# Global value rows of batches 2 and 3: from the DMA of each tile instead of a VectorE copy

## The chip, the core and the metric

The kernel runs on one core of a Trainium2 chip. The metric is device time in microseconds (us): 718.45 us, the median of three runs (717.41 to 722.96).

## What is computed

Attention over 4 batches, 8 heads, 512 local and 32 global tokens, head size 64, followed by two mixture-of-experts layers with 8 experts each. The change lies in attention. A local query attends to the 32 global keys and to the local keys at most 32 positions away:

```python
s_ll = scale * np.matmul(q_l, k_l.transpose(0, 1, 3, 2))
mask = np.abs(pos[:, None] - pos[None, :]) <= window          # window = 32
s_ll = np.where(mask, s_ll, -1000000000.0)
s_lg = scale * np.matmul(q_l, k_g.transpose(0, 1, 3, 2))
a_l = sm(np.concatenate([s_lg, s_ll], axis=-1))
out_l = np.matmul(a_l, np.concatenate([v_g, v_l], axis=2))
```

Global queries attend to everything. The 2176 token rows of 512 values then go through `_moe_ref` and `_moe2_ref`: each row is sent to the expert with the largest logit, `out[mask] = gate_w * (max(x @ w1[e], 0) @ w2[e])`.

## The kernel before

**Tiles and steps.** A local tile is 128 queries of one batch, all 8 heads; batch b has tiles 4b to 4b+3 (n = 4b + qb). Each tile is two work items, one for the even and one for the odd heads (`hg` 0 and 1), and each batch has two items of global queries (`Global`) after its first local tile (in batch 0 after its second). One Python loop over t writes all engines' instructions in order; `tc.manual_schedule()` keeps that order on every engine. In step t the item t computes its scores (matmuls to `s_`), item t-2 has its probabilities transposed (`turn`, to `pt`, copied to `pT` by ScalarE), item t's scores get their row maxima on VectorE (`soften`: `amx` and `anm` for a local tile, `mg` and `gnm` for global queries) and their exponentials on ScalarE (`pe`, `pg`), item t-3 is multiplied with the values (`values`, to `po` or `og`), item t-4's row is turned for the router (`ptx`), and router pieces follow (`pp`, `sp`, `pl`, `lg`, `at`). So TensorE, VectorE and ScalarE pass work round within each step.

**The value window.** For a tile, `vw` holds for each of 4 groups of 32 queries (`cg`) 128 value rows: two end blocks of 32 rows, 32 global rows and so on, ordered so that the even groups have end block and global rows in partitions 0 to 63 and the odd groups in 64 to 127. Three buffers `vws` are used in turn, tile n has `vws[n % 3]`. `load_windows` issues two SyncE DMAs (even groups, odd groups), which bring 32 end-block rows for two groups each, and four GpSimd copies of 64 rows from the batch's value tile. `global_values` brings the 32 global rows, by two VectorE copies from `vg`, where all batches' global values lie. Tiles 0 to 2 get them by DMA, with 64 rows for each group. Tiles 4 to 6, 8 to 10 and 12 to 14 get them by these copies. The fourth tile of a batch (3, 7, 11, 15) finds them in its buffer, which the first tile of the batch used.

**When.** After the second half of tile n-3's `values`, `load_windows` for tile n is written, and the two copies of `global_values` follow, one at the end of this step and one at the end of the next (`take(1, filling)`). Tile 12 is an exception: in step 28 its load is put behind the four loads of the first expert's `w1a` on the SyncE queue (`load1`, 512 KB each), which wait for the choice of the first expert (`first`). The second half of those weights (`w2a`) is loaded in steps 31 and 32.

Of the kernel before, what the change touches and what calls it, by code (L numbers as in the profile page):

```python
# [20 lines left out]
P = 128  # L21
# [31 lines left out]
def start_block(g):  # L53
    return (3 * g) // 2 if g % 2 == 0 else (3 * g + 1) // 2
# [51 lines left out]
def sparse_attention_two_moe(ctx, tc, qt, kt, vx, vn, qg, emb, tau, w1a, w2a, wgo, w1b, w2b, cs1, cs2, out):  # L106
# [65 lines left out]
    def take(n, *its):  # L172

        for _ in range(n):
            for it in its:
                next(it, None)
# [18 lines left out]
    def embed_turn(psp):  # L195
        pe_ = psp.tile([P, 4, 8], F32, name="pe_", tag="small")
        for k in range(4):
            T.transpose(pe_[:, k, :], em[:, k * P:(k + 1) * P], ident[:E, :E])
        V.tensor_copy(enT[:, :, :8], pe_)

    def zero_rows():

        G.memset(order[1].oh, 0.0)
        G.memset(order[1].rank, 0)
        G.memset(at[:, SMAIN:SMAX, :], 0.0)
        for i in range(2):
            G.dma_start(out=xs[i][ZROW:ZROW + 1, :], in_=zt[0:1, :])
            G.dma_start(out=gs[i][ZROW:ZROW + 1, :], in_=zrow)
        for i in range(SMAIN, SMAX):
            G.dma_start(out=xs[1][row0(i, 1):row0(i, 1) + P, :], in_=zt)  # L210
            G.dma_start(out=gs[1][row0(i, 1):row0(i, 1) + P, :], in_=zt[:, :2])
# [429 lines left out]
    def rows_of(a, n):  # L641
        return [a[:, k * n:(k + 1) * n] for k in range(4)]
# [10 lines left out]
    def keep_warm(n, psp):  # L653

        if n:
            warm = psp.tile([P, 512], F32, name="idle", tag="small")
            for i in range(n):
                T.matmul(warm, lhsT=onesb, rhs=ones, start=True, stop=True)
# [849 lines left out]
    def load_batch(b):  # L1508
        kq = big()
        kT = kq[:, :4 * EXT].rearrange("p (j n) -> p j n", j=4)  # L1510
        qT = kq[:, 4 * EXT:].rearrange("p (j n) -> p j n", j=4)
        if b == 0:

            S.dma_start(out=qT[:, :, :2 * P], in_=qt[b, :, :, :2 * P].rearrange("j p n -> p j n"))
            for k0, k1 in ((0, 288), (288, EXT)):
                SP.dma_start(out=kT[:, :, k0:k1], in_=kt[b, :, :, k0:k1].rearrange("j p n -> p j n"))
                yield
            SP.dma_start(out=qT[:, :, 2 * P:], in_=qt[b, :, :, 2 * P:].rearrange("j p n -> p j n"))
        else:
            G.dma_start(out=kT, in_=kt[b].rearrange("j p n -> p j n"))  # L1520
            G.dma_start(out=qT, in_=qt[b].rearrange("j p n -> p j n"))
        held[b] = (kT, qT)
        yield

    def load_values(b):

        if b == B - 1:  # L1530
            room = gp.tile([P, 4, DM], F32, name="room")
            halves_ = [room[:, :2], room[:, 2:]]
        elif b == 2:
            halves_ = [st2[i] for i in range(2)]
        else:
            halves_ = [st1[2 * b + i].rearrange("p (j d) -> p j d", j=2) for i in range(2)]
        held[b, "v"] = [a[:, j, :] for a in halves_ for j in range(2)]
        for i, a in enumerate(halves_):
            (G if b else SP).dma_start(out=a, in_=vn[b, :, 2 * i:2 * i + 2])
            yield  # L1540

    def load_windows(b, qb):

        n = 4 * b + qb
        vw = vws[n % 3]
        for par in range(2):
            r0 = start_block(4 * qb + par) * 32  # L1550
            p0, p1 = ((P - 64, P) if par else (0, 64)) if n < 3 else ((96, P) if par else (0, 32))
            SP.dma_start(out=vw[p0:p1, par:4:2, :], in_=strided(vx[b], r0 + p0, p1 - p0, 96, 2))
        v = held[b, "v"][qb]
        for cg, to, of in ((0, 64, 0), (1, 0, 0), (2, 64, 64), (3, 0, 64)):
            G.tensor_copy(vw[to:to + 64, cg, :], v[of:of + 64])
        held[b, qb] = vw
# [7 lines left out]
    def strided(rows_, r0, n, step, m):  # L1564

        a = rows_[r0:r0 + n, :]
        return bass.AP(tensor=a.tensor, offset=a.offset, ap=[a.ap[0], [step * DM, m], a.ap[1]])
# [163 lines left out]
    for b in range(B):  # L1731
        loc = [("L", b, qb, hg) for qb in range(4) for hg in range(2)]
        n = 2 if b else 4
# [28 lines left out]
    for t in range(len(items) + 3):  # L1762
        if t - 7 in routes:
            routes[t - 7][0].gather(routes[t - 7][1])
        if t < len(items):
            it = items[t]
            if it[0] == "G":
                live[t] = live[t - 1].second if it[2] else Global(it[1])
            else:
                b, qb, hg = it[1:]  # L1770
                if hg == 0:
                    sums = sm.tile([P, H], F32, name="sums", bufs=3)
                if hg == 0 and qb == 0 and 0 < b < B - 1:
                    take(1, load_batch(b + 1))
                    take(2, load_values(b + 1))
                live[t] = Local(b, qb, hg, live[t - 1] if hg else None, sums)
            live[t].scores()
        if t < 6:
            keep_warm(3, ps_m)
        if 2 <= t < 6:  # L1780
            take(4, emb_norm)
        if t == 4:
            for i in range(1, 3):
                SP.dma_start(out=vg[i * SG:(i + 1) * SG, 1:], in_=vx[1:, 32:64, :].rearrange("b p d -> p b d"))
        if t == 22:
            SP.dma_start(out=wg[:, :, :16], in_=wgo.rearrange("p (k e) -> p k e", k=4))
            zero_rows()
        if t == 6:
            embed_turn(ps_m)
            V.tensor_copy(trib, d[:, C_TRI:C_TRI + P])  # L1790
            V.tensor_copy(order[0].val, d[:, C_VAL:C_VAL + len(TILES)])
            V.tensor_copy(order[0].gt[:, :, 1], d[:, C_TOK:C_TOK + len(TILES)])
        if t == 28:
            chosen = first.choose(acc1, ps_m, "small")
            take(1, chosen)
        if t == 32:
            take(1, found)
            first.rows = row0(8)
        if t - 2 in live:
            live[t - 2].turn()  # L1800
        if t < len(items):
            live[t].soften()
        if 28 <= t < 31:
            take(1, chosen)
        if t == 28:
            first.load()
        if t - 3 in live:
            done = live.pop(t - 3)
            r = done.values()
            if r is not None:  # L1810
                routes[t - 3 + 3 * isinstance(done, Global)] = r
            if t == len(items) + 2:
                groups[3].norm2()
            if not isinstance(done, Global) and done.hg == 1:
                n = done.b * 4 + done.qb + 3
                if 4 <= n < 16 and n % 4 < 3:
                    filling = global_values(n // 4, n % 4)
                if t == 28:

                    awaited = n // 4, n % 4  # L1820
                elif n < 16:
                    load_windows(n // 4, n % 4)
        if t == 28:
            load1(w1a, first.ex)
            load_windows(*awaited)
        elif t in (31, 32):
            load2(w2a, first.ex, range(2 * t - 62, 2 * t - 60))
        if t - 4 in routes:
            routes[t - 4][0].turn(routes[t - 4][1])
            routes[t - 4][0].store_rows(routes[t - 4][1])  # L1830
        if t - 5 in routes:
            routes[t - 5][0].multiply(routes[t - 5][1])
        take(1, filling)
        if t == 31:
            found = first.find(range(8), ps_m, "small", 8)
            take(1, found)
        if t == 31:
            w1h = rows_of(big().bitcast(F32R), F)
        if 31 <= t < 35:
            G.tensor_copy(w1h[t - 31], st1[t - 31])  # L1840
        if t == 35:
            sl[0].gather(0)
            sl[0].gather_gate(0)
        if t == 36:
            gx.close()
            wp = ctx.enter_context(tc.tile_pool(name="wp", bufs=1, side="right"))
            w2h = [wp.tile([P, 2, DM], F32R, name=f"w2h{k}") for k in range(4)]
            w2l = []
            sl[0].xT = wp.tile([P, 4, P], F32, name="xT0")
        if t == 40:  # L1850
            w1l = rows_of(big().bitcast(F32R), F)
        if t == 40:
            sl[0].turn_first()
            halves = sl[0].mm1_parts()
        if t == 42:
            take(2, halves)
        if t == 39:
            V.tensor_copy(groups[4].xr[0], xg)
        order[0].mark(1)
        stages(t, t == len(items) + 1)  # L1860
# [119 lines left out]
```

## Time and profile before

| | us |
|---|---|
| median of 3 runs (lowest, highest) | 718.45 (717.41, 722.96) |
| the profiled execution | 717.52 |
| its span, first to last instruction | 715.7 |
| TensorE busy | 642.1 (90%) |
| VectorE busy | 424.0 (59%) |
| ScalarE busy | 366.1 (51%) |
| GpSimd busy | 212.6 (30%) |
| mean granted TensorE clock | 0.969 of full speed |

PE is TensorE's matmuls and PEld its weight loads, DVE is VectorE, ACT ScalarE, POOL GpSimd, and SPq the queue on which SyncE issues DMAs. A bracket at the end of a timeline row gives the idle time of the engine just before it and what ended it; "issue" stands where the engine waited for nothing that the profile shows. Attention ends at about 155 us: the last `po` matmul starts at 153.5 us. Everything after it is the two expert layers. Batches 2 and 3 of attention stand between about 70 and 155 us.

### The profile page before, as it was taken

How to read it: one execution, taken by the hardware profiler on the slowest of the kernel's cores; microseconds unless marked ns; L12 is line 12 of the kernel's file. 1: busy time of each engine (PE TensorE's matmuls, PEld its weight loads, DVE VectorE, ACT ScalarE, POOL GpSimd, SP SyncE). 2: the span in 40 equal slices, each digit the busy share in tenths (PEclk: the TensorE clock that was granted, in tenths of full speed). 3: DMA queues.
4: the chain of work that ended last, by engine and by line, in shares of the span. 5: the costliest groups of instructions: out<-in, count | busy, mean ns of one | idle time of the engine just before them, and what ended most of it. 6: DMA issues, size and time to landing. Idle time of an engine off the chain costs nothing. (4 is left out here: it accounts for less than half of the span.)

```text
span 715.7 us, 20133 instructions
## 1 busy us (share of the span) xinstructions
PE 642.1 (90%) x6255; PEld 513.0 (72%) x6263; DVE 424.0 (59%) x1210; ACT 366.1 (51%) x885; POOL 212.6 (30%) x292
## 2 busy tenths in 40 slices
PE   7787775887899989989898988989999999999994
PEld 3465554654878878868786777668887988788883
DVE  3567869668515666368667776772574555474350
ACT  2676767662424724256358654332674544474540
POOL 3452644403712122122220230032233334324131
PEclk9989989899999999999999999999999999999998
DMA  9975848423247613655586444524757444735400
GB/s 268 270 272 174 287 102 231 146 61 63 62 150 210 209 60 72 211 181 168 146 268 158 142 149 134 163 75 142 290 188 246 161 164 167 264 122 211 148 24 28
DMA packets 55290, 117.88 MB, mean 165 GB/s; under 512 B 13815, under 2 KB 15607, under 8 KB 55104
## 3 DMA queue, kind: packets, MB, share of 16 engines
q1 hardware_dynamic: 44688, 87.21, 38.8%
q0 software_dynamic: 9344, 27.91, 12.5%
q8 instruction: 86, 1.41, 0.8%
q14 instruction: 100, 0.82, 0.6%
q10 hardware_dynamic: 1072, 0.53, 0.3%
HBM read 100.11 MB, written 16.30 MB: 163 GB/s over the span
## 5 line engine op out<-in xcount | busy, mean ns | idle before, releaser
L646 DVE TENSOR_TENSOR kq<-st,kq 128x1024 fp32r<-128x1024 f32 x64 | 75.2, 1219 | 64.3 <-ACT kq L769 53.8
L1097 PE MATMUL py<-w2h,hh 128*128 128x512 f32 x304 | 88.7, 413 | 0.0
L1097 PE MATMUL py<-w2l,hh 128*128 128x512 f32 x304 | 83.2, 394 | 0.4 <-DVE w2l L646 0.4
L646 DVE TENSOR_TENSOR w2l<-st,w2h 128x1024 fp32r<-128x1024 f32 x64 | 74.1, 1218 | 12.3 <-ACT w2h L769 8.0
L684 POOL DMA_INDIRECT xrow<-xs,idx x40 | 51.7, 1294 | 59.6 <-DVE ge L582 42.9
L957 PE MATMUL ph<-kq,xh 128*128 128x512 f32 x256 | 64.4, 405 | 4.1 <-DVEq L848 1.0
L1097 PEld LDWEIGHTS py<-w2l,hh 128*128 128x128 f32 x304 | 56.9, 188 | 14.6 <-DVE w2l L646 1.3
L1169 POOL DMA_INDIRECT out<-yr,ti x21 | 23.6, 1123 | 145.5 <-issue 34.9
L1097 PE MATMUL py<-w2h,hl 128*128 128x512 f32 x232 | 63.5, 395 | 0.0
L684 POOL DMA_INDIRECT gt<-gs,idx x40 | 53.1, 1328 | 19.1 <-issue 8.9
L957 PEld LDWEIGHTS ph<-kq,xh 128*128 128x128 f32 x256 | 48.1, 192 | 14.5 <-issue 1.1
L769 ACT CAST kq<-st 128x1024 fp32r<-128x1024 f32 x56 | 55.9, 1047 | 4.5 <-ACTq L744 2.6
L769 ACT CAST w2h<-st 128x1024 fp32r<-128x1024 f32 x56 | 54.5, 1049 | 5.6 <-ACTq L831 2.0
L1097 PEld LDWEIGHTS py<-w2h,hh 128*128 128x128 f32 x304 | 51.7, 189 | 7.3 <-ACT w2h L769 0.2
L902 PE MATMUL ph<-xh,kq 128*128 128x256 f32 x384 | 50.7, 293 | 5.9 <-ACTq L761 3.1
L700 POOL TENSOR_SCALAR va<-gt 128x1 f32<-128x1 f32 x21 | 5.2, 247 | 167.8 <-DVE oh L1203 167.4
L1111 ACT ACTIVATE yr<-py,gt 128x512 f32<-128x512 f32 x38 | 26.1, 688 | 54.1 <-PE py L1097 30.2
L902 PEld LDWEIGHTS ph<-xh,kq 128*128 128x128 f32 x384 | 48.5, 200 | 7.1 <-ACTq L761 3.7
L902 PE MATMUL pht<-xh,kq 128*128 128x256 f32 x384 | 48.2, 281 | 4.4 <-DVEq L761 2.3
L1097 PEld LDWEIGHTS py<-w2h,hl 128*128 128x128 f32 x232 | 43.5, 188 | 10.4
L902 PEld LDWEIGHTS pht<-xh,kq 128*128 128x128 f32 x384 | 45.4, 188 | 6.9 <-ACTq L761 2.9
L989 ACT COPY hs<-ph 128x512 f32<-128x512 f32 x32 | 17.2, 590 | 56.5 <-PE ph L999 29.6
(544 smaller groups left out, 1278.1 us busy)
## 6 DMA issues: line engine op xcount, KB each, us to landing
st<-in_w1a SPq DMA_DIRECT2D x32, 512.0 KB
st<-in_w2a SPq DMA_DIRECT2D x32, 512.0 KB
st<-in_w1b SPq DMA_DIRECT2D x32, 512.0 KB
st<-in_w2b SPq DMA_DIRECT2D x32, 512.0 KB
xs<-yr SPq DMA_DIRECT2D x21, 256.0 KB
kq<-in_kt POOLq DMA_DIRECT2D x3, 1728.0 KB, 9.3
xs<-xrow SPq DMA_DIRECT2D x17, 256.0 KB
vw<-in_vx SPq DMA_DIRECT2D x26, 128.0 KB
```

The costliest lines, as they stand in the source:

```text
L646: eng.tensor_sub(lo[k], st[k], hi[k].bitcast(F32))
L684: G.indirect_dma_start(out=to, out_offset=None, in_=rows_[self.l][:n, :], in_offset=bass.IndirectOffsetOnAxis(ap=idx, axis=0), bounds_chec ...
L700: G.tensor_scalar(out=self.va[s], in0=tok, scalar1=FAR, scalar2=None, op0=ALU.is_lt)
L769: S.copy(hi[k], st[k])
L902: T.matmul(po, lhsT=w[k][:, f * P:(f + 1) * P], rhs=x[:, k, at], start=first and k == 0 and f % 2 == 0, stop=last and k == 3, skip_group_c ...
L957: T.matmul(ph[n], lhsT=x[:, k, s % XR], rhs=ws[k][n][part], start=first and k == 0, stop=last and k == 3, skip_group_check=True)
L989: S.copy(self.h[s][n], ph[n])
L1097: T.matmul(py, lhsT=hT[k][x], rhs=w[k // 2][:, k % 2], start=first and k == 0, stop=k == 7, skip_group_check=True)
L1111: S.activation(yr, py, AF.Copy, scale=gate)
L1169: G.indirect_dma_start(out=out, out_offset=bass.IndirectOffsetOnAxis(ap=self.ti.pop(s), axis=0), in_=yr, in_offset=None, bounds_check=NTOK ...
```

## The change

For tiles 8, 9, 10, 12, 13 and 14 `load_windows` lets each of its two DMAs bring 64 partitions instead of 32 (end block and global rows, which lie side by side in `vx`), and `global_values` is called for tiles 4, 5 and 6 alone.

```diff
-            p0, p1 = ((P - 64, P) if par else (0, 64)) if n < 3 else ((96, P) if par else (0, 32))
+            whole = n < 3 or 8 <= n and qb < 3
+            p0, p1 = ((P - 64, P) if par else (0, 64)) if whole else ((96, P) if par else (0, 32))
             SP.dma_start(out=vw[p0:p1, par:4:2, :], in_=strided(vx[b], r0 + p0, p1 - p0, 96, 2))
...
-                if 4 <= n < 16 and n % 4 < 3:
+                if 4 <= n < 7:
                     filling = global_values(n // 4, n % 4)
```

On VectorE, in step 30 and 31 (tile 13's copies; `xrow` is the finished row of tile 10, `fb`, `so` and `fto` belong to the search for the first expert's rows, `lg` to the router, `mg` to the global scores of batch 3), before:

```order
L1633 TENSOR_TENSOR xrow<-po,rs 128x512
L234 COPY sp_2354<-pp_2349 128x128
L1561 COPY vw_180<-vg 32x2x512
L276 TENSOR_SCALAR at<-d,pf,val_102 128x128
L1561 COPY vw_180<-vg 32x2x512
L457 TENSOR_TENSOR fb<-oh_99,fone 128x64
L459 TENSOR_REDUCE so<-fb 128x8
```

and with the change (its lines from 1552 on have numbers higher by one):

```order
L1634 TENSOR_TENSOR xrow<-po,rs 128x512
L234 COPY sp_2346<-pp_2341 128x128
L276 TENSOR_SCALAR at<-d,pf,val_102 128x128
L457 TENSOR_TENSOR fb<-oh_99,fone 128x64
L459 TENSOR_REDUCE so<-fb 128x8
```

The two copies are gone and the order of the rest is the same. This is so at all twelve places.

On the SyncE queue, in steps 28 to 30 (`st` takes the expert's weights, `vw_179` is tile 12's window and `vw_180` tile 13's), before:

```order
L219 DMA st_3_93<-in_w1a 128x1024
L1552 DMA vw_179<-in_vx 32x2x512 x2
L400 DMA gs_68<-gt_103 128x4x2
L405 DMA xs_66<-xrow 128x512
L1552 DMA vw_180<-in_vx 32x2x512 x2
```

and with the change:

```order
L219 DMA st_3_93<-in_w1a 128x1024
L1553 DMA vw_179<-in_vx 64x2x512 x2
L400 DMA gs_68<-gt_103 128x4x2
L405 DMA xs_66<-xrow 128x512
L1553 DMA vw_180<-in_vx 64x2x512 x2
```

Each of these DMAs has 64 partitions in place of 32; the order is unchanged. TensorE, ScalarE and GpSimd keep their order too.

## Rows read from the trace of the kernel before

**Rows 1.** The page, part 1: busy time, share of the span, instructions

```profile
PE 642.1 (90%) x6255; PEld 513.0 (72%) x6263; DVE 424.0 (59%) x1210; ACT 366.1 (51%) x885; POOL 212.6 (30%) x292
```

**Rows 2.** Instructions of line 1561: count, ns min/median/max, first and last start, shape

```profile
L1561 DVE COPY vw<-vg x18: 683/684/1008, 33.2 to 124.3; 32x1024 f32<-32x1024 f32 x18
```

**Rows 3.** Timeline of VectorE, 74 to 88 us: start, us, line, operation, idle before

```profile
74.07 0.80 DVE L1561 COPY vw<-vg 32x1024 f32<-32x1024 f32 x1
...
75.15 0.68 DVE L1601 TENSOR_REDUCE amx<-s__1514 128x4 f32<-128x512 f32 x1
...
81.16 0.68 DVE L1670 TENSOR_REDUCE mg<-s__1647 128x1 f32<-128x512 f32 x1
...
87.93 0.28 DVE L1691 COPY pgT<-t2g 32x128 f32<-32x128 f32 x1 [1.84 <-PE t2g L1687]
```

**Rows 4.** Timeline of TensorE and ScalarE, 74 to 86 us

```profile
74.81 0.66 PE L1615 MATMUL pt<-ident,pe 128*128 128x128 f32 x4 [0.35 <-ACT pT L1617]
...
83.06 0.69 ACT L1678 ACTIVATE pg<-s__1647,gnm 128x512 f32<-128x512 f32 x1 [0.84 <-DVE gnm L1673]
...
85.10 0.66 PE L309 MATMUL ptx<-ident,xrow 128*128 128x128 f32 x4 [1.59 <-ACT pg L1679]
```

**Rows 5.** Timeline of TensorE, 89 to 99 us

```profile
89.96 0.30 PE L232 MATMUL pp<-xT,enT 128*32 128x128 f32 x1 [1.18 <-issue]
...
94.62 0.31 PE L1701 MATMUL og<-st,pgT 128*32 128x64 f32 x5
...
98.34 1.07 PE L1701 MATMUL og<-st,pgT 128*32 128x64 f32 x27 [3.42 <-issue]
```

**Rows 6.** Stretches: length; PE, PEld, DVE, ACT, POOL busy; PEclk; DMA; GB/s

```profile
88.00:90.00 2.00, 0.82 (x40) 0.54 (x32) 1.85 (x6) 0.76 (x3) 0.54 (x1) 1.00 1.06 338
...
98.00:100.00 2.00, 1.66 (x43) 1.23 (x42) 0.16 (x1) 1.44 (x9) 0.00 (x0) 0.50 0.01 3
```

**Rows 7.** Timeline of VectorE, 112 to 129 us

```profile
112.08 0.68 DVE L1601 TENSOR_REDUCE amx<-s__2261 128x4 f32<-128x512 f32 x1
...
116.78 0.68 DVE L1561 COPY vw<-vg 32x1024 f32<-32x1024 f32 x1
...
117.84 0.69 DVE L1561 COPY vw<-vg 32x1024 f32<-32x1024 f32 x1
...
123.61 1.71 DVE L1561 COPY vw<-vg 32x1024 f32<-32x1024 f32 x2
...
128.57 0.28 DVE L1691 COPY pgT<-t2g 32x128 f32<-32x128 f32 x1 [3.05 <-PE t2g L1687]
```

**Rows 8.** Timeline of TensorE, 111 to 125 us

```profile
111.37 0.65 PE L1615 MATMUL pt<-ident,pe 128*128 128x128 f32 x4
...
119.60 0.34 PE L465 MATMUL pi<-fto,at 128*128 128x1 f16 x8 [0.90 <-DVE lg L324]
...
121.75 0.30 PE L1625 MATMUL po<-vw,pT 128*32 128x64 f32 x2
...
122.57 0.65 PE L1625 MATMUL po<-vw,pT 128*32 128x64 f32 x30 [0.52 <-DMA vw<-in_vx]
...
124.37 0.66 PE L309 MATMUL ptx<-ident,xrow 128*128 128x128 f32 x4 [1.16 <-ACT pg L1679]
```

**Rows 9.** Timeline of the SyncE queue, 109 to 112 us

```profile
109.20 2.14 SPq L219 DMA_DIRECT2D st<-in_w1a  x4
...
111.45 0.97 SPq L1552 DMA_DIRECT2D vw<-in_vx  x2
```

**Rows 10.** Stretches of 2 us, the same columns, 112 to 122 us

```profile
112.00:114.00 2.00, 2.00 (x77) 1.47 (x76) 1.97 (x5) 0.99 (x4) 1.22 (x2) 1.00 1.05 391
...
118.00:120.00 2.00, 1.10 (x42) 0.80 (x27) 1.49 (x7) 0.51 (x2) 0.00 (x0) 1.00 1.58 210
...
120.00:122.00 2.00, 2.00 (x50) 1.36 (x48) 1.93 (x7) 0.58 (x1) 0.34 (x1) 1.00 0.58 77
```

**Rows 11.** The page, part 3: queue, kind, packets, MB, share of 16 engines

```profile
q8 instruction: 86, 1.41, 0.8%
```

## The prediction

> **What bounds the kernel now.** The page's busy times come first: TensorE is busy for 642.1 us [rows 1], nearly the whole run, and most of that is the expert layers, which the change does not touch. A microsecond that attention ends earlier or later should therefore move the end by a microsecond. So I looked at the list of line 1561's instructions and then at the timelines of batches 2 and 3, engine by engine, for what TensorE waits for there. The reader is to see that it is fed in turns: VectorE's row maxima free ScalarE's exponentials, and these free the next turn on TensorE. At two places it waits for something else, a pause with no visible cause and the window load of tile 12; both are taken up below.
>
> **What goes.** Line 1561 has 18 copies with a median of 684 ns [rows 2]. Twelve go, two for each of tiles 8, 9, 10, 12, 13 and 14: 12 × 0.684 = 8.2 us of VectorE, 1.1% of the run. That is the ceiling of what the copies alone can give, if each stood on the path to the end. Their places say how many do.
>
> *Tiles 8 and 9.* Tile 8's second copy runs at 74.07 for 0.80 us, and the maxima of the next scores start at 75.15 [rows 3]. They could not have started before these scores were done. TensorE starts its next work at 74.81 after 0.35 us of idle [rows 4], so the scores ended by 74.46, and removing the pair gains 75.15 - 74.46 = 0.69 us, not 1.4. Tile 9's two copies stand ahead of the global maxima at 81.16 [rows 3]. These release ScalarE's `pg` at 83.06, which had then been idle for 0.84 us [rows 4]; before that ScalarE was at work on what the first 0.69 us also advance. So tile 9's pair (2 × 0.684 = 1.37 us) gives at most these 0.84. TensorE's `ptx` at 85.10 had waited 1.59 us for `pg` [rows 4], and it takes the whole 0.69 + 0.84 = **1.53 us**.
>
> *The pause behind it.* TensorE then stops in the middle of a group: 5 matmuls of `og`, 3.42 us of nothing, then the other 27 [rows 5]. A smaller stop of 1.18 us precedes it [rows 5]. The profile names no one who ended either. If these stops stay where they are in TensorE's own order, they move with it and the 1.53 us survive. If they last until the transfers ahead of them are through, the gain is swallowed, and the added bytes of tiles 9 and 10 make it worse: 4 DMAs × 131,072 B (32 partitions × 2 groups × 2048 B each) at the 338 GB/s of that time [rows 6] are 524,288 / 338,000 = 1.55 us. The two ends are thus -1.53 and +1.55. I take -1.53, because the 1.18 us stop ended inside the stretch 88 to 90 us with the DMA share at 1.06 [rows 5, 6], with transfers still running. Against it stands that by 98 to 100 us, where the long stop ends, the share is 0.01 [rows 5, 6].
>
> *Tiles 12 and 13.* VectorE's maxima at 112.08 [rows 7] wait behind tile 12's copies; their scores ended by about 111.4, where TensorE goes on with `pt` at 111.37 [rows 8], so 0.7 us is to be had. Tile 13's copies, at 116.78 and 117.84 [rows 7], hold up `lg`, for which TensorE waits 0.90 us before 119.60 [rows 8]. Together TensorE would come to tile 12's values 0.7 + 0.9 = 1.6 us earlier, at 121.75 - 1.6 = 120.15.
>
> *What waits there.* Tile 12's load stands on the SyncE queue at 111.45, behind four loads of 512 KB from 109.20 on [rows 9], and it is already late. TensorE does two matmuls of `po` at 121.75 and then stops for 0.52 us, until the window is in, at 122.57 [rows 8]. The start of these loads is set by the choice of the first expert, ahead of which no copy of batch 3 stands, so it doesn't move against the steps around it. The load now carries 262,144 B more. No row has the price, so I bound it by the GB/s of the stretches around: 0.67 us at 391, 3.40 us at 77, and 1.16 us at the mean of 391, 210 and 77 [rows 10], which is 226. I take 1.16, because the load is in flight through all three. A gain is excluded for the load itself, as no byte leaves the queue. TensorE then resumes at 122.57 + 1.16 = 123.73 and is through after 0.65 us at 124.38, just when `ptx` starts today (124.37, after 1.16 us of waiting for ScalarE [rows 8]). ScalarE's side comes 1.6 us earlier and no longer binds. So tile 12's window takes the place of that wait, and this stretch gives 0.0 us, between -0.48 (at 391) and +2.25 (at 77).
>
> The Trainium skill, page "DMA: Bandwidth & Descriptors", section "Specifications", gives a core about 358 GB/s from HBM; as an estimate from that page the bytes cost 0.73 us and the stretch gives -0.42 us, so the sum below would be 715.6 instead of 716.0. The stretch at 77 GB/s [rows 10] is far below that figure while this load is still out, so I do not use it.
>
> *Tiles 10 and 14.* Both pairs lie in front of an idle stretch of VectorE. After tile 14's pair, at 123.61 us, it idles 3.05 us until a transpose of TensorE is done [rows 7], and after tile 10's it idles 1.84 us before the row at 87.93 us [rows 3]. These four copies are worth 0; if the idle were gone they would be worth 2.7.
>
> *The other five loads.* Each carries 262,144 B more as well. Tiles 9, 10, 13 and 14 are loaded in steps 20, 22, 30 and 32 and used seven steps later, tile 12 only five. Tile 8 has five too, but no weights stand before it on the queue. I cost them at nothing; what hides them is this distance, and without it each would cost what tile 12's does. The stores of rows and the `w2a` loads behind them on the queue come later by about the same microsecond, and nothing in attention waits for those.
>
> **The sum.** -1.53 + 0.0 = -1.5 us against the profiled execution's own 717.52: 716.0. The median of the runs, 718.45, lies 0.93 higher, so I put the changed kernel's median at **716.9 us**.
>
> **Rivals.**
> *Slower: the added bytes take more than the copies gave* (0.26). They do it in the long stop, which would then end when the transfers do, and at tile 12's load. With +1.55 there and 0 to +2.25 at tile 12 the run takes 718.45 + 1.55 = 720.0 to 722.3 us. It decides from the point where the stop grows by more than the 1.53 us that TensorE gained. For it: the DMA share of 1.06 [rows 6], the queue of instruction transfers, which goes through the same engines [rows 11], and the wait already seen at tile 12. After the long stop the granted clock is 0.50 [rows 6], the 1.2 GHz level, so a longer stop may cost more than its length. Against it: the 1.18 us stop. The Trainium skill ("DMA: Bandwidth & Descriptors", section "Queues, rings and completion order") says that a DMA engine takes turns between queues packet by packet; by that rule other queues' bytes would slow an instruction transfer but not hold it to their end, and 716.9 to 719.2 would be left of this rival. The DMA share of 0.01 at the stop's end [rows 6] neither bears it out nor refutes it.
>
> *More is gained* (0.17). The added bytes go beside others and tile 12's load comes no later than TensorE; then the 1.16 us of `ptx` are gained too: 718.45 - 1.53 - 1.16 = 715.8. If the long stop of 3.42 us also shrinks to the 1.18 of the other, 2.24 more: 713.5. For it: the share around tile 12 falls to 0.58 [rows 10], so there is room. Against it: the load is late already.
>
> *Nothing moves* (0.12). What VectorE saves is waited for elsewhere at each place: 718.45, give or take 0.5. That the change doesn't do what it says is excluded by the order of the instructions, where the twelve copies are gone and the twelve DMAs are twice as tall.
>
> **Chances and range.** My forecast has 0.45. A measurement of this kernel can tell about 1% from no change, 7.2 us: below 711.3 or above 725.6. All copies together could give 8.2, and only with the long stop and its slow clock gone as well would the time come near 711: 0.04. For over 1% slower a second stop of 3.4 us and the full 2.25 at tile 12 would have to come on top of 1.55: 0.03. Within 1%: 0.93. The range reaches from the shrunken stop, 713.5, to the slower rival's upper part, 722.0.
>
> **What would show it.** In the changed kernel's trace, line 1561 (then 1562) has 6 copies. `pg` of batch 2 starts without the 0.84 us of idle, and the `ptx` after it comes 1.5 us earlier. The stop in `og` keeps about 3.4 us; if it is longer and ends with the last transfers, the slower rival is right. At tile 12 TensorE's wait for `vw` grows from 0.52 to about 0.52 + 1.6 + 1.16 = 3.3 us and the wait of the next `ptx` for `pg` is gone; a wait of under 1 us there would prove the bytes harmless. The forecast is wrong if the first expert layer starts no earlier than it does now, or if it starts earlier and the end doesn't follow.

## The result, and the profile after

The change makes the kernel slower by two thirds of a per cent: 722.02 us, the median of 20 runs (719.07 to 727.09), against 717.96 of 20 runs of the kernel before (711.23 to 722.96). The ratio is 1.0066, with a 95% interval of 1.0044 to 1.0087; on 717.96 us that is 4.7 us, between 3.2 and 6.2. The forecast had been a gain of 1.5. The profiled execution took 724.72 us, 7.2 more than the one before. 1.9 of these are there at the end of attention (the last `po` ends at 155.7 us, before at 153.8); whether the expert layers lose too, or these two executions only happen to differ there, is taken up under "Attention by itself".

The page says that the change did what it says: VectorE has 12 instructions and 9.8 us less than in [rows 1].

```profile
span 722.8 us, 20129 instructions
...
PE 647.5 (90%) x6263; PEld 516.0 (71%) x6263; DVE 414.2 (57%) x1198; ACT 366.7 (51%) x885; POOL 204.1 (28%) x292
...
q8 instruction: 86, 1.41, 0.8%
```

Line 1562 (1561 before; all lines from 1552 on are one higher) has only the six copies of tiles 4 to 6 left:

```profile
L1562 DVE COPY vw<-vg x6: 681/838/1008, 32.4 to 52.7; 32x1024 f32<-32x1024 f32 x6
```

What did that buy? On VectorE (start, duration, operation, idle before and releaser) the maxima that stood behind the copies in [rows 3] now wait for TensorE:

```profile
76.04 0.69 DVE L1602 TENSOR_REDUCE amx<-s__1512 128x4 f32<-128x512 f32 x1 [1.10 <-PE s__1513 L1591]
...
81.42 0.69 DVE L1671 TENSOR_REDUCE mg<-s__1643 128x1 f32<-128x512 f32 x1 [0.50 <-PE s__1643 L1656]
...
87.23 0.17 DVE L324 COPY lg<-pl 128x8 f32<-128x8 f32 x1 [2.64 <-PE pl L323]
```

By the clock these rows are later than 75.15 and 81.16 in [rows 3]. But this execution was late already: TensorE started the twelfth group of 32 `po` matmuls, which lies ahead of every instruction that the change touches, at 71.49 us instead of 69.95 (first before, then after):

```profile
69.95 0.65 PE L1625 MATMUL po<-vw,pT 128*32 128x64 f32 x32
71.49 0.65 PE L1626 MATMUL po<-vw,pT 128*32 128x64 f32 x32
```

Counted from that group, the first maxima start at 4.55 us instead of 5.20 and those of the global scores at 9.93 instead of 11.21: 0.65 and 1.28 us earlier, and now VectorE idles where it copied. ScalarE's `pg` has 0.28 us of idle ahead in place of 0.84 [rows 4], and from the group it is 1.27 us earlier (11.84 instead of 13.11):

```profile
83.33 0.69 ACT L1679 ACTIVATE pg<-s__1643,gnm 128x512 f32<-128x512 f32 x1 [0.28 <-DVE gnm L1674]
```

And this is TensorE in the same stretch; the first row is the whole `po` group as it ran before, all others are after:

```profile
82.86 0.65 PE L1625 MATMUL po<-vw,pT 128*32 128x64 f32 x32
...
83.69 0.53 PE L1626 MATMUL po<-vw,pT 128*32 128x64 f32 x21
86.06 0.41 PE L1626 MATMUL po<-vw,pT 128*32 128x64 f32 x11 [1.84 <-issue]
86.41 0.66 PE L309 MATMUL ptx<-ident,xrow 128*128 128x128 f32 x4
...
89.67 0.42 PE L232 MATMUL pp<-xT,enT 128*32 128x128 f32 x7
93.07 0.30 PE L232 MATMUL pp<-xT,enT 128*32 128x128 f32 x1 [2.99 <-issue]
...
98.93 0.31 PE L1702 MATMUL og<-st,pgT 128*32 128x64 f32 x5
100.04 0.64 PE L1702 MATMUL og<-st,pgT 128*32 128x64 f32 x27 [0.80 <-issue]
```

In [rows 4] `ptx` waited 1.59 us for `pg`. That wait is gone, as forecast. But one group earlier TensorE now stops for 1.84 us in the middle of `po`, where it had not stopped, waiting for nothing that the profile names. The stop in `pp` has grown from 1.18 to 2.99 us and that in `og` has shrunk from 3.42 to 0.80 [rows 5]. The three together are 4.60 us before and 5.63 after. At tile 12 it looks like this, with the load on the SyncE queue below it:

```profile
120.36 0.30 PE L1626 MATMUL po<-vw,pT 128*32 128x64 f32 x2
124.42 0.65 PE L1626 MATMUL po<-vw,pT 128*32 128x64 f32 x30 [3.76 <-DMA vw<-in_vx]
125.00 0.67 PE L309 MATMUL ptx<-ident,xrow 128*128 128x128 f32 x4
```

```profile
109.47 2.14 SPq L219 DMA_DIRECT2D st<-in_w1a  x4
111.71 1.43 SPq L1553 DMA_DIRECT2D vw<-in_vx  x2
```

TensorE comes to tile 12's values at 120.36 instead of 121.75 us, the load lets it go on at 124.42 instead of 122.57 [rows 8], and the load was issued only 0.26 us later than in [rows 9]. The stretches (length, busy time of PE, PEld, DVE, ACT, POOL, granted clock, DMA share, GB/s) show TensorE standing still at a DMA share of about 1, and its clock at the 1.2 GHz level after the long wait:

```profile
84.00:86.00 2.00, 0.22 (x15) 0.06 (x3) 0.58 (x2) 1.79 (x9) 0.00 (x0) 1.00 1.02 296
90.00:92.00 2.00, 0.09 (x3) 0.00 (x0) 1.84 (x6) 1.04 (x6) 0.00 (x0) 1.00 1.06 406
122.00:124.00 2.00, 0.00 (x0) 0.00 (x0) 0.27 (x2) 1.03 (x5) 1.94 (x3) 1.00 0.92 139
126.00:128.00 2.00, 2.00 (x66) 1.50 (x64) 0.12 (x1) 0.92 (x3) 0.00 (x0) 0.50 1.04 359
```

### The profile page after: what moved, and what is told of

Same layout as the page of the kernel before. It is cut to its first block, busy times and chain, and to the rows that moved or that the text cites. A ratio compares the mean times of both kernels' runs of the same rounds, so it can differ in the third digit from the quotient of the medians.

```text
span 722.8 us, 20129 instructions
## 1 busy us (share of the span) xinstructions
PE 647.5 (90%) x6263; PEld 516.0 (71%) x6263; DVE 414.2 (57%) x1198; ACT 366.7 (51%) x885; POOL 204.1 (28%) x292
## 3 DMA queue, kind: packets, MB, share of 16 engines
q8 instruction: 86, 1.41, 0.8%
## 5 line engine op out<-in xcount | busy, mean ns | idle before, releaser
L1097 PE MATMUL py<-w2l,hh 128*128 128x512 f32 x304 | 83.8, 396 | 0.5 <-DVE w2l L646 0.5
L957 PE MATMUL ph<-kq,xh 128*128 128x512 f32 x256 | 66.8, 416 | 3.6 <-ACT zs L1220 1.5
L957 PEld LDWEIGHTS ph<-kq,xh 128*128 128x128 f32 x256 | 49.9, 200 | 14.5 <-ACT zs L1220 1.7
L902 PE MATMUL ph<-xh,kq 128*128 128x256 f32 x384 | 49.0, 286 | 5.7 <-ACTq L761 2.9
L684 POOL DMA_INDIRECT gt<-gs,idx x40 | 47.4, 1184 | 20.0 <-issue 9.8
L902 PEld LDWEIGHTS ph<-xh,kq 128*128 128x128 f32 x384 | 46.8, 194 | 7.1 <-ACTq L761 3.7
```

Source lines behind the costliest of these rows:

```text
L684: G.indirect_dma_start(out=to, out_offset=None, in_=rows_[self.l][:n, :], in_offset=bass.IndirectOffsetOnAxis(ap=idx, axis=0), bounds_chec ...
L902: T.matmul(po, lhsT=w[k][:, f * P:(f + 1) * P], rhs=x[:, k, at], start=first and k == 0 and f % 2 == 0, stop=last and k == 3, skip_group_c ...
L957: T.matmul(ph[n], lhsT=x[:, k, s % XR], rhs=ws[k][n][part], start=first and k == 0, stop=last and k == 3, skip_group_check=True)
L1097: T.matmul(py, lhsT=hT[k][x], rhs=w[k // 2][:, k % 2], start=first and k == 0, stop=k == 7, skip_group_check=True)
```

## First experiments: tile 12, the bytes, the copies

The largest new wait is that of 3.76 us at tile 12. Theory A1 says that it is the loss. A2 says that the loss is in the other loads, those of tiles 8 to 10 above all; A, without a number, is the added bytes wherever they hurt. C says that taking the copies away costs the time, by moving what follows on VectorE. D says that attention is innocent and the expert layers behind it run worse. Each expectation says what its theories give.

**t12copy** brings tile 12's global rows by copies again:

```diff
-            whole = n < 3 or 8 <= n and qb < 3
+            whole = n < 3 or 8 <= n and qb < 3 and n != 12
...
-                if 4 <= n < 7:
+                if 4 <= n < 7 or n == 12:
```

> The change, but tile 12 gets its global rows by VectorE copies as before, so the load that stands behind the first expert's weights carries its old bytes. Theory A1 (the wait for tile 12's window, 0.52 us before and 3.76 us after, is the loss) expects the wait under 2 us and 717 to 718.5. Theory A2 (the bytes of tiles 8 to 10, loaded while batch 3's inputs arrive, stretch the stops of TensorE between 84 and 100 us) expects 721 to 722.

Measured: 720.50 us, the median of 12 runs (one of them took 1527.04 us and is not in the ratio); ratio to the kernel before 1.0050 [1.0021, 1.0079], which is 3.6 us. TensorE's wait for the window is 1.07 us:

```profile
124.75 0.65 PE L1626 MATMUL po<-vw,pT 128*32 128x64 f32 x30 [1.07 <-DMA vw<-in_vx]
125.32 0.66 PE L309 MATMUL ptx<-ident,xrow 128*128 128x128 f32 x4
```

**after_first** is the changed kernel with tile 12's load ahead of the first expert's four loads on the queue:

```diff
+            load_windows(*awaited)
...
-            load_windows(*awaited)
```

> The change, with tile 12's window load put ahead of the first expert's four w1a loads on the SyncE queue. Theory A1 expects the wait of TensorE for tile 12's window to vanish and the time to fall to 716 to 718. Theory A2 expects it to vanish too, but the time to stay at 720 to 722.

Measured: 721.70 us (6 runs), 1.0097 [1.0060, 1.0135], which is 7.0 us. The wait for tile 12 is gone and `ptx` waits for `pg` again, 1.59 us:

```profile
120.09 0.65 PE L1626 MATMUL po<-vw,pT 128*32 128x64 f32 x32
122.33 0.66 PE L309 MATMUL ptx<-ident,xrow 128*128 128x128 f32 x4 [1.59 <-ACT pg L1680]
```

The time did not fall with it, in either kernel to the 716 to 718.5 us that A1 expected. A1 falls: the most visible wait of the new profile is not what the change costs.

**bytes_only** has the tall DMAs and keeps all copies (those of batches 2 and 3 write to rows of the global values' tile that nobody reads). Its edit to the changed kernel:

```diff
-            V.tensor_copy(vws[(4 * b + qb) % 3][at_, par:4:2, :], vg[at_, b, None, :].to_broadcast((SG, 2, DM)))
+            to = vg[at_, 0:2, :] if b > 1 else vws[(4 * b + qb) % 3][at_, par:4:2, :]
+            V.tensor_copy(to, vg[at_, b, None, :].to_broadcast((SG, 2, DM)))
...
-                if 4 <= n < 7:
+                if 4 <= n < 16 and n % 4 < 3:
```

> The DMAs bring 64 partitions as with the change, and VectorE still does the twelve copies, with the same sources and size, into rows of vg that nobody reads. Theory A expects the whole loss and more, since TensorE no longer comes early: 722 to 725. Theory C expects no loss: about 718.

Measured: 720.53 us (12 runs) against 717.50: 1.0060 [1.0026, 1.0093]. By that ratio the bytes alone cost 4.3 us, between 1.9 and 6.7: nearly three times what the whole change was to gain, and not C's "no loss". TensorE here still waits for `pg`, and stops in `pp` and `og`, but not in `po`:

```profile
83.85 0.66 PE L309 MATMUL ptx<-ident,xrow 128*128 128x128 f32 x4 [1.20 <-ACT pg L1681]
...
90.13 0.42 PE L232 MATMUL pp<-xT,enT 128*32 128x128 f32 x1 [2.61 <-issue]
...
98.33 0.64 PE L1703 MATMUL og<-st,pgT 128*32 128x64 f32 x27 [2.08 <-issue]
```

**nocopy** drops the copies and adds no byte; its edit to the kernel before:

```diff
-                if 4 <= n < 16 and n % 4 < 3:
+                if 4 <= n < 7:
```

> The twelve VectorE copies are left out and the DMAs bring 32 partitions as before, so the windows of tiles 8 to 14 keep the global rows of batch 1: this part of the result is left out. Theory A (the loss comes from the added bytes) expects what the copies are worth alone: 1.5 to 3 us faster than before, about 715 to 716.5. Theory C (the loss comes from removing the copies, by moving everything that follows on VectorE) expects about 722, as with the change.

Measured: 733.61 us, 1.0241 [1.0192, 1.0290]. Its windows hold the global rows of an earlier batch, so other rows go to other experts, and its time says nothing of the copies. Its attention does, which has the same instructions: the stop in `po` is there with no byte added.

```profile
85.66 0.41 PE L1625 MATMUL po<-vw,pT 128*32 128x64 f32 x11 [1.86 <-issue]
...
91.85 0.30 PE L232 MATMUL pp<-xT,enT 128*32 128x128 f32 x1 [2.16 <-issue]
```

## Attention by itself

To keep the expert layers out, four kernels end behind attention; the finished rows are copied to the output and both expert layers are left out:

```diff
-    s0.open()
...
-            s0.steps(0, SMAIN, sl[1])
+    SP.dma_start(out=out[:ZROW, :], in_=xs[0][:ZROW, :])
+    SP.dma_start(out=out[ZROW:NTOK, :], in_=xs[0][ZROW + 1:NTOK + 1, :])
```

cut_before, cut_after, cut_nocopy and cut_bytes are the kernel before, the change, nocopy and bytes_only so cut.

> The kernel before, with everything after attention, routing and the first slot's products left out: both expert layers' slots are missing and the routed rows are copied out as they are. It is the reference for the next three, which are cut at the same place. No theory differs on it; about 185 to 200 us.

> The changed kernel cut at the same place, both expert layers left out. Theory A (the added bytes cost time in attention itself) expects 4 to 5 us more than cut_before, the whole loss. Theory D (attention comes out even, and the loss arises in the expert layers, which the change does not touch in the code) expects within 1 us of cut_before.

> As cut_before, without the twelve copies and without added bytes (stale global rows for tiles 8 to 14, so that part of the result is left out; with the expert layers cut off, the other routing costs nothing). Both theories expect the worth of the copies alone here: the forecast's 1.53 plus 1.6, some 3 us less than cut_before.

> As cut_before, with the taller DMAs and the twelve copies kept as dummies. Theory A expects 4 us or more over cut_before, at least as much as cut_after. Theory D expects within 1 us.

Measured, medians of 6 runs: cut_before 192.46 us (187.48 to 196.31), cut_after 196.36 (192.29 to 197.00, and one run of 233.64), cut_nocopy 191.52 (189.26 to 196.21), cut_bytes 195.96 (193.23 to 199.01). A loss of 3.9 us is there without the expert layers, where D had said 1 at most; between the lowest runs it is 4.8. The bytes alone make 3.5 by the median and 5.8 by the lowest run. Leaving out the copies alone gives 0.9 by the median and loses 1.8 by the lowest run, where some 3 of gain were expected: it cannot be told from nothing. With a spread of 3 us to either side, these are signs and not sizes.

The whole kernels' traces tell the same of D. From attention's last `po` to the end it takes 562.0 us before and 567.1 after, but 562.4 in bytes_only, 561.0 in t12copy, 562.0 in after_first and 563.6 in pool, whose expert layers have the same code. The 5 us there belong to the one profiled execution of the changed kernel, and D falls.

## Which tiles, and is it the program's length?

One thing disturbed the picture. TensorE reaches the twelfth group of 32 `po` matmuls (the second half of tile 5) at 70.0 us before and 71.5 after, and so it went by kernel: late without VectorE's copies, early with them. Theory L puts this and the loss down to the number of VectorE's instructions. **cut_tiny** is cut_after with twelve copies of one column in the old places:

```diff
+            to = vg[at_, 0:2, :1] if b > 1 else vws[(4 * b + qb) % 3][at_, par:4:2, :]
+            V.tensor_copy(to, vg[at_, b, None, :to.shape[-1]].to_broadcast((SG, 2, to.shape[-1])))
...
+                if 4 <= n < 16 and n % 4 < 3:
```

> cut_after (both expert layers left out) with twelve one-column VectorE copies at the places of the old ones, into rows that nobody reads, so that VectorE's program is as long as before at next to no time. In the traces so far the four kernels with twelve copies reach TensorE's 12th group of value products at 66.1 to 66.6 us and the six without at 67.8 to 69.3, ahead of every changed instruction. Theory L (the shorter VectorE program shifts its instruction fetches, and that costs some 2 us) expects 66 to 66.6 there and 194 to 195 in all. Theory A (bytes alone) expects 67 to 69 by chance and 196, as cut_after.

The expectation's 66 to 69.3 us are the times of the group before it, the eleventh by the count used here. Measured: 194.77 us (4 runs), which is L's time but inside the scatter of cut_after; the eleventh group at 68.1 us and the twelfth at 71.8: late, with as many of these copies as bytes_only has. L, which needs it early, falls.

**cut_b2** and **cut_b3** make the change for tiles 8 to 10 or 12 to 14 alone (cut_b2 shown):

```diff
+            whole = n < 3 or 8 <= n < 11
...
+                if 4 <= n < 7 or 12 <= n < 15:
```

> The cut kernel (both expert layers left out) with the change for tiles 8, 9 and 10 alone. Theory A2 (the bytes hurt where batch 3's inputs arrive) expects 195.5 to 196.5, the whole loss. Theory A1 (they hurt behind the first expert's weights) expects 191.5 to 193.

> The cut kernel (both expert layers left out) with the change for tiles 12, 13 and 14 alone. Theory A1 expects 195 to 196.5, theory A2 192 to 193. If both halves show about 194, the loss is spread over all the loads.

Measured: 194.56 us (189.96 to 199.54) and 192.94 (190.24 to 196.03), 2.1 and 0.5 above cut_before. The medians point to tiles 8 to 10, but the lowest runs lie 2.5 and 2.8 above that of cut_before: this does not tell the two halves apart.

**pool** is the whole kernel with small DMAs and the twelve copies on GpSimd, the version that by theory A should have beaten both:

```diff
-            V.tensor_copy(vws[(4 * b + qb) % 3][at_, par:4:2, :], vg[at_, b, None, :].to_broadcast((SG, 2, DM)))
+            (G if b > 1 else V).tensor_copy(vws[(4 * b + qb) % 3][at_, par:4:2, :], vg[at_, b, None, :].to_broadcast((SG, 2, DM)))
```

> The whole kernel, with the DMAs as before and the twelve copies made by GpSimd instead of VectorE: VectorE is relieved of the same work and no byte is added. Theory A expects a gain of 1 to 3 us over the kernel before, ratio 0.996 to 0.999. Theory L (fewer VectorE instructions cost 2 us by themselves) expects no gain, 0.999 to 1.002.

Measured: 718.66 us against 718.24, 0.9989 [0.9950, 1.0028]: VectorE freed, not a byte added, and no gain seen. The interval, from -3.6 to +2.0 us, excludes neither nothing nor the forecast's 1.5.

## Bytes or a late start

Four cut kernels were to part the bytes (theory B, the A2 of above) from the late start (theory S): cut_before and cut_after once more, tall DMAs for tiles 8 to 10 with all copies kept, and pool cut off. The edit of cut_b2bytes to the cut kernel before:

```diff
+            whole = n < 3 or 8 <= n < 11
...
+            to = vg[at_, 0:2, :] if b == 2 else vws[(4 * b + qb) % 3][at_, par:4:2, :]
...
```

> The kernel before, cut off at the end of attention (both expert layers left out; the rows go to the output as they are). The base of this comparison; 192.5 us the first time. Theory B (the added bytes cost the time) and theory S (the programs without VectorE's full copies start some 2.3 us later, before anything changed is reached) say the same of it: 191 to 194 us. If the early shift is a draw of chance of each run, TensorE's value products of step 18 will not stand at 69.7 us again but anywhere between 69 and 73.

> The changed kernel, cut off at the end of attention (expert layers left out); 196.4 us the first time. Theory B: slower than the cut kernel before by 3 to 4 us, of which the part behind step 18 (69 to 72 us) is at least 2. Theory S: slower by 2 to 3 us, all of it ahead of step 18, and the part behind it the same within 1 us. Neither: no difference over 1 us, and the loss of the first comparison was scatter.

> The cut kernel before with the tall DMAs of tiles 8, 9 and 10 alone; every copy stays on VectorE (those of these three tiles write two rows of the global values' own tile that nobody reads). 6 x 131,072 B more, no copy less. Theory B: the bytes of tiles 8 to 10 are the price, so slower than the cut kernel before by 2 to 3.5 us, with longer stops of TensorE between 66 and 105 us. Theory S: the copies are all there, so no early shift and no loss: within 1 us of the cut kernel before.

> The cut kernel before with the twelve copies of batches 2 and 3 issued on GpSimd in place of VectorE, no byte added. Theory B: no bytes, so not slower than the cut kernel before, and up to 1.5 us faster. Theory S: VectorE's copies are gone, so the early shift is there and it is slower by 1 to 2.5 us than the cut kernel before.

Measured, 6 runs each: cut_before2 190.38 us (187.55 to 192.59), cut_after2 195.69 (191.67 to 201.34), cut_b2bytes 194.06 (191.84 to 198.38), cut_pool 193.62 (190.71 to 195.17). The base is 2.1 us lower than the same kernel was the first time, so only differences within this set count. In cut_b2bytes six taller DMAs and nothing else cost 3.7 us (4.3 between the lowest runs): B is borne out, and S, which said under 1, fails there. In cut_pool, with no byte, the median and the lowest run are 3.2 us higher, as S and not B said: its trace reaches the twelfth group at 70.9 us against 68.7 in cut_before2, and takes 79.5 us from there against 79.9. That loss is not firm, since the same edit lost nothing in the whole kernel (pool). In cut_after2 the part behind that group takes 84.8 us, where S wanted the 79.9 within 1. So neither theory holds alone. TensorE's waits in total (line, releaser: us, times, longest) between 66 and 160 us show what the bytes do, first cut_before2, then cut_b2bytes:

```profile
PE pp L232 <- issue: 1.8, 1, 1.8
...
PE og L1701 <- issue: 0.9, 1, 0.9
```

```profile
PE pp L232 <- issue: 3.1, 1, 3.1
...
PE po L1627 <- issue: 1.1, 2, 0.9
PE og L1703 <- issue: 1.0, 1, 1.0
```

The stops without a named cause in these groups grow from 2.7 us to 5.2, and one in `po` is among them, though the copies are there.

## What the stops are

The stops stand at the same few instructions in all kernels. Counted in TensorE's matmul records, those of the changed kernel come after the 1615th (in `po`), the 1742nd (in `pp`) and the 1869th (in `og`): 127 apart. t12copy and after_first add the places 1488, 2376, 2503 and 2631, on the same grid of about 127. Two more, 981 and 1108, lie ahead of the twelfth group; all 18 traces stop at one of these or at both, for 0.2 to 3.5 us together, so such stops are no work of the change. Each matmul has one weight load (6263 of each on the page after), so the grid is about 255 instructions. The queue of instruction transfers [rows 11] moved 1.41 MB in 86 transfers, 16.4 KB each; over 255 instructions that is 64 B apiece. In attention it keeps step: from 62.60 to 151.14 us of the changed kernel there are 15 transfers from start to start and 1840 matmuls. (The expert layers bring more transfers than that rate would give; why, no run here shows.) And the start of the last transfer of this queue before TensorE goes on is, in the changed kernel and in the one before:

```
            transfer starts    TensorE goes on    between
after            83.55              86.06           2.51
after            90.50              93.07           2.57
after            97.50             100.04           2.54
before           87.45              89.96           2.51
before           95.38              98.34           2.96
```

Over all 18 traces there are 43 stops at these three places, and 42 of them end 2.2 to 3.1 us after such a start (one after 3.7). By the count, the size and the time together, the stops are TensorE waiting for the next piece of its own program.

What makes them long is when a transfer starts. In the changed kernel the DMA share is 0.04 to 0.37 between 62 and 74 us, and 0.80 to 1.08 from 76 to 98. After the places 1108, 1235 and 1362, in the first stretch, the next transfer starts 0.2 to 1.8 us after TensorE has entered a piece (in 53 of 54 cases over all traces; in one it starts 0.4 before). After 1488, 1615 and 1742, in the second, it starts 2 to 6 us after. Once started it takes no longer: 0.9 to 1.6 us (median 1.2) between 57 and 72 us, 0.9 to 2.2 (median 1.1) between 74 and 100. So in this stretch a transfer is not slower under load but starts late; what in the load holds it back is not shown. (At tile 12's load, from 116 to 123 us, single transfers were slow: 3.09 us in the kernel before, 3.56 at most over all traces.) The changed kernel's TensorE went through the three pieces from 65.03 to 78.67 us in 4.0 to 5.0 us each, and the transfers at 62.60, 66.12 and 70.18 kept to that, some 4 us apart. From 75.94 to 97.50 they come 7.2 us apart. There TensorE cannot be faster than its program arrives.

That makes a measure with less scatter than the whole time: the three intervals between the 11th and the 14th transfer (75.94 to 97.50 in the changed kernel), while the windows of tiles 8 to 10 are loaded. "Copies" and "bytes" mean VectorE's full copies and the added bytes of these three tiles (cut_tiny's copies of one column count as none):

| | three intervals, us, by trace | mean |
|---|---|---|
| copies, no bytes: before, cut_before, cut_before2, cut_b3 | 21.2, 21.4, 19.2, 18.7 | 20.1 |
| neither: nocopy, cut_nocopy, pool, cut_pool | 19.9, 19.1, 21.3, 19.5 | 19.9 |
| both: bytes_only, cut_bytes, cut_b2bytes | 22.5, 22.0, 22.6 | 22.4 |
| bytes, no copies: after, cut_after, cut_after2, t12copy, after_first, cut_tiny, cut_b2 | 21.6, 21.5, 24.0, 22.2, 21.5, 20.8, 21.3 | 21.8 |

The bytes add about 2 us here, with or without copies, over a scatter of 1 us from trace to trace. The late starts after 1488, 1615 and 1742 say the same: together 11.6 us on the mean of the eight traces without the bytes, 13.4 on that of the ten with them. The copies' going adds or takes nothing that can be seen in the sum: this stretch runs at the pace of the transfers. Within the sum it moves a transfer: the first interval is 6.1 to 6.7 us in the four kernels of the first row and 7.7 to 9.1 in those of the second, and the other two are shorter. So the stop in `po` stands in all eleven kernels without the full copies, in two of the three with copies and bytes, and in none of the four with copies alone. Why that transfer starts later without the copies is not shown. cut_pool is the plainest case. It has neither copies nor bytes, and the stops are where they were, the one in `po` new:

```profile
85.69 0.41 PE L1625 MATMUL po<-vw,pT 128*32 128x64 f32 x11 [2.02 <-issue]
...
92.07 0.37 PE L232 MATMUL pp<-xT,enT 128*32 128x128 f32 x1 [2.36 <-issue]
```

The rest of the comparison comes from the same traces. From the twelfth group to attention's last `po`, the three kernels before of the first row take 83.8, 80.7 and 79.9 us (mean 81.5), the first three changed ones of the last row 84.2, 83.7 and 84.8 (84.2): 2.7 us. Over all traces it is 80.7 on the mean without these bytes (78.0 to 83.8) and 83.5 with them (82.5 to 84.8). The twelfth group itself is reached at 70.0, 69.7 and 68.7 against 71.5, 73.8 and 70.1 (means 69.5 and 71.8): 2.3 us. Together 5.0, beside a measured 4.7. All seven kernels with the full copies of tiles 8 to 10 reach the group at 68.5 to 70.3, the eleven others at 70.1 to 73.8. The second part is thus seen in every kernel, and **not explained**: no instruction or transfer of the change comes before it, and cut_tiny shows that the number of instructions is not it. The stops at 981 and 1108 make up little of it: 2.1 us on the mean of the seven, 2.7 on that of the eleven. What the change costs behind it is shown; why the start is late stays open.

Put together, attention's last `po` ends at 150.9 us on the mean of the three kernels with copies and no byte, at 151.1 for the four with neither, at 153.3 for the three with both and at 155.2 for the seven with bytes and without copies. Behind the twelfth group the four with neither take 79.8 us against 81.5: a sign, from few traces, that the copies' going does give something there, and that the late start takes it back.

## Why the prediction was wrong

- **The copies.** Twelve went, as said, and up to `pg` the forecast nearly held. Tile 8's 0.69 us came: from the twelfth group to the maxima it takes 5.20 us in all seven kernels with the full copies and 4.55 in ten of the eleven others (3.84 in cut_after), because the maxima now start when the scores are done. Of tile 9's 0.84 us ahead of `pg`, 0.56 came, so `pg` is 1.27 us earlier, and TensorE's 1.59 us for it went. But from the group to `ptx` it took 85.10 - 69.95 = 15.15 us before and 86.41 - 71.49 = 14.92 after: 0.23 of the 1.53 was left. The new stop in `po` had taken the rest.
- **The step that failed: "if these stops stay where they are in TensorE's own order, they move with it and the 1.53 us survive".** They do stay at their places in its order, but they end some 2.5 us after a transfer starts, and a TensorE that gets there sooner only stands longer. The prediction took the profile's "issue" for a pause that keeps its length. It also had nothing for a place that showed no stop, the one in `po`. Counted from the twelfth group, TensorE came to that place 0.7 us sooner with the change, but the transfer that it needed there started at 12.06 us (83.55) instead of 10.38 (80.33), and it stood for 1.84 us. At the end of the stop in `og` all of the gain was gone: 28.55 us from the group instead of 28.39. The reason given for the choice (the stop of 1.18 us ended with transfers still running) was no reason: the transfer that ended it began at 87.45 us and took 1.18 us in the midst of the others. It need not wait for their end; it had started late.
- **"The other five loads" cost nothing: wrong.** The prediction looked for who waits for a window. Nobody waits for those of tiles 8 to 10, but their bytes share the engines with TensorE's program: 2 us in the three intervals, 3.7 us in cut_b2bytes, 4.3 us for the run by bytes_only, which has the bytes of tiles 12 to 14 as well.
- **Tile 12.** Forecast: TensorE 1.6 us earlier, the load 1.16 later, a wait of 3.3, the wait for `pg` gone, the stretch at 0.0. Measured: 1.39 earlier, 1.85 later, 3.76, gone, and `ptx` at 125.00 against 124.37, 0.63 us. From the load's own issue, which came 0.26 us later, it is 1.65 earlier, 1.59 later and 0.37. That was mechanism and nearly size; the 1.16 us was too low. after_first shows that it is not what decides.
- **The rival "slower"** had the queue of instruction transfers as its reason and 720.0 to 722.3 as its price; the run took 722.02. Its places were off: the stop in `og` shrank, those in `po` and `pp` grew, and nearly half of the 5.0 us lies in the late start, which it did not have. That the price fits is in part luck.
- **Two rules weighed.** The Trainium skill ("DMA: Bandwidth & Descriptors", "Queues, rings and completion order") has a DMA engine take turns between queues by packets. The traces agree that a transfer is not held to the others' end; that turns slow it they show at most around tile 12's load (3.09 us in the kernel before, at a share of 1.58), not at the three stops of the changed kernel, where it took 1.02 to 1.11 us at a share near 1, as at rest. There it is the start that is late. The prediction took from the rule that little would be left of the rival; no run shows that, and here a transfer comes every 127 matmuls. The skill's page "Runtime: NRT & Kernel Launch" ("Instruction fetch mechanics") says that instructions come in 16 KiB blocks of 256 and that crossing a block is mostly hidden. The 16.4 KB and the grid of about 127 pairs agree; the 43 stops of 0.4 to 3.4 us say that at a DMA share near 1 it is not hidden.

## What to carry to other kernels

Where a busy TensorE stops in the middle of a group for "issue", count its instructions between such stops: if the count repeats and the instruction queue starts a transfer just before each stop ends, it is waiting for its program, and such a stop takes back what the work ahead gains. In such a stretch, moving work from an engine with idle time to DMA gained nothing here and cost the bytes, even where nobody waits for the data itself. And take the most visible new wait out before blaming it: the one at tile 12 went away and the time stayed.

## What had not been expected of the hardware

TensorE's program came in pieces of 16.4 KB, one for about 127 matmuls with their weight loads, through the same DMA engines as the data. A piece's transfer began 2.2 to 3.1 us before TensorE went on. From 57 to 100 us it took 0.9 to 2.2 us, as long at rest as under load, but started 0.2 to 1.8 us after TensorE had entered the piece ahead with the DMA engines nearly at rest, and 2 to 6 us after at a share near 1. 262,144 B more on a load that was already queued let TensorE go on 1.85 us later at tile 12 (1.59 from the load's issue), with stretches at 139 to 210 GB/s just ahead, and not the 0.7 us that the best stretch of [rows 10] would give.
